# A spectral filter's weights, read four neighbours at a time

## The chip, the cores and the metric

The kernel runs on one core of a Trainium2 chip. The metric is the time of one launch on the device, in microseconds. Each engine (TensorE for matmuls, VectorE, ScalarE, GpSimd, SyncE for the DMA queue) works through its own list of instructions in order and waits on semaphores for the others. The kernel before takes 224.96 us (median of 3 runs, 224.48 to 225.21).

## The reference

One input `x` of 2048 rows by 640 columns (bfloat16) goes two ways after a layer norm, and the result is the sum of both and `x`:

```python
x = A_x
xn = layernorm(x)
X = rfft2(xn) * (w_r + 1j * w_i)          # 2048 x 321 complex filter weights
A = irfft2(X)
B = ((xn @ w_gate) * (xn @ w_up)) @ w_down   # 640 -> 1536 -> 640
out = x + A + B
```

The filter weights `w_r` and `w_i` lie in memory in the natural order of the 321 frequencies of a row.

## The kernel before, in words

The Fourier transforms are matmuls with tables of cosines and sines. The rows are split as 32 x 64 and the columns as 10 x 64, and the factor 5 of the columns is done in a few additions on VectorE. The work is cut into named tasks, and a planner written in the kernel (`_Sched.plan`) lays them out from their dependencies, priorities and estimated durations: it chooses the order on every engine, for some copies the engine too, and the PSUM banks. The estimates are those in the `task` calls; the instructions themselves are made by the functions named `em_...`. The eight PSUM banks are given out singly or in pairs; a task that reads a bank last gives it back.

The stages, roughly in this order: layer norm and transposes (T0); S, R: row additions and the first matmuls; then 16 steps t = 0 to 15, each over a group of 128 row frequencies, of which the change touches nearly all parts; then I, V: the way back, 16 groups; last the down projection (ACC, line 1141), to which the inverse transform (IV, line 1149) is added in PSUM, the sum with `x` (FIN, line 1156), and the stores. The gate and up projections (GU, line 923, ten matmuls each), their copies out of PSUM (eG) and products (H, line 938, on VectorE) have lower priority on TensorE and fill its gaps up to the end of the 16 steps and some way behind them.

One step t:

- `ld_w`: four DMAs on SyncE's queue bring 128 rows of `w_r` and of `w_i` into one of four slots.
- D (line 964, TensorE): five matmuls into a pair of PSUM banks. Column frequencies are computed as four groups k of 64, each with its real and imaginary part c, and a last group of 65 that stands for the multiples of five.
- eD (line 704, the helper that copies; ScalarE for nearly all t): PSUM to a bfloat16 row of 2 x 321, in the order c, k, m.
- C (lines 985 to 988, TensorE): four matmuls of 321 columns, along the rows.
- WM (VectorE): each of the two parts of C times `w_r` and `w_i`. Four multiplies of 256 elements (line 1000) and one of 260 (line 1003). Within a group k the 64 frequencies m come in two halves h. Frequency (k, m) of the first half is element 10 m + k + 1 of a weight row, and of the second half element 10 m + 9 - k; so neighbours along m lie ten weights apart.
- CB (lines 1018 to 1022, VectorE): sum and difference of the products to the complex result, written as bfloat16. NG (lines 1028 to 1030, ScalarE): its negated or swapped copy, so that `v_y` holds, for each k, the blocks -im, re' and im of 64 side by side.
- IA (lines 1041 and 1042, TensorE): for each of five k two matmuls, whose stationary operand is 128 neighbouring columns of `v_y`. eIA (line 704) copies the result to `v_z2w`.

The products `v_p` and `v_y` have two slots each, the rows of eD three. So C of step t waits for CB of step t-2, and IA waits for NG of its step.

In the tables below, line 704 is the line of the copy helper for ScalarE and 705 the one for VectorE; they hold the copies of all stages. Line 698 is the helper that issues DMAs.

Of the kernel before, what the change touches and what calls it, by code (L numbers as in the profile page):

```python
# [495 lines left out]
_ACTF = mybir.ActivationFunctionType  # L496
_OP = AluOpType
# [47 lines left out]
def _build(nc, A_x, A_w_r, A_w_i, B_w_gate, B_w_up, B_w_down, out, opts=None):  # L545
# [3 lines left out]
    with es:  # L549
# [64 lines left out]
        ps = es.enter_context(nc.psum_tensor("ps", [128, 8, 512], _F32))  # L614
# [14 lines left out]
        v_w = V("W").rearrange("p (r w l) -> p r w l", r=_NW, w=2)  # L629
# [5 lines left out]
        v_ti = V("TI").rearrange("p (t c n) -> p t c n", t=16, c=2)  # L635
# [14 lines left out]
        v_p = V("P").bitcast(_F32).rearrange("p (r w c l) -> p r w c l", r=2, w=2, c=2)  # L650
# [51 lines left out]
        def copy_on(c, dst, src):  # L702
            if c.e is nc.scalar:
                return c.e.activation(dst, src, _ACTF.Copy)  # L704
            return c.e.tensor_copy(dst, src)
# [241 lines left out]
        for t in range(16):  # L947
            pq = 10.0 + 0.05 * t
            ar = t % 3
            r2 = t % 2  # L950
            wr = t % _NW
            for w_ in range(2):
                for h in range(2):
                    k2 = int(_rows(t, 0, h, 0))
                    dma("ld_w%d_%d_%d" % (t, w_, h), v_w[64 * h:64 * h + 64, wr, w_, 0:321], wvs[w_][:, k2, :],
                        64 * 642, [(b_w, ("r", 4 * wr + 2 * w_ + h, 4 * wr + 2 * w_ + h + 1))], prio=9.5 + 0.05 * t,
                        semkey=("w", wr), after=[wpad])

            def em_d(c, t=t):
                bk = bank_of(c.t)  # L960
                ins = None
                for k in range(5):
                    n = 128 if k < 4 else 130
                    ins = c.e.matmul(psflat[:, bk * 512 + k * 128: bk * 512 + k * 128 + n], v_uq[:, k, t, :],
                                     v_fd[:, k * 128: k * 128 + n], start=True, stop=True)
                return ins
            td = T("D_%d" % t, "pe", 5 * _d_mm(128), em_d, reads=[(b_u, None), (b_fd, None)],
                   prio=pq, bank="pair", cls="a")

            def em_ed(c, td=td, ar=ar):  # L970
                bk = bank_of(td)
                src = psflat[:, bk * 512: bk * 512 + 642]
                dst = v_a[:, ar, :].rearrange("p (c n) -> p c n", c=2)
                copy_on(c, dst[:, :, 0:256].rearrange("p c (k m) -> p k c m", k=4),
                        src[:, 0:512].rearrange("p (k c m) -> p k c m", k=4, c=2))
                return copy_on(c, dst[:, :, 256:321], src[:, 512:642].rearrange("p (c m) -> p c m", c=2))
            ed = T("eD_%d" % t, ("act", "dve"), {"dve": _d_dve_psum(512) + _d_dve_psum(130), "act": _d_act(512) + _d_act(130)}, em_ed,
                   writes=[(b_a, ("r", ar, ar + 1))], prio=pq - 0.001, frees=td)
            hold(td, ed)

            def em_c(c, t=t, ar=ar):
                bk = bank_of(c.t)
                a_r = v_a[:, ar, 0:_LP]
                a_i = v_a[:, ar, 324:324 + _LP]
                c.e.matmul(ps[:, bk, 0:_LP], v_tf[:, t, 0, :], a_r, start=True, stop=False)
                c.e.matmul(ps[:, bk + 1, 0:_LP], v_tf[:, t, 0, :], a_i, start=True, stop=False)
                c.e.matmul(ps[:, bk, 0:_LP], v_tf[:, t, 1, :], a_i, start=False, stop=True)
                return c.e.matmul(ps[:, bk + 1, 0:_LP], v_tf[:, t, 2, :], a_r, start=False, stop=True)
            tc = T("C_%d" % t, "pe", 4 * _d_mm(_LP), em_c, reads=[(b_a, ("r", ar, ar + 1)), (b_tf, ("t", t, t + 1))],
                   prio=pq, bank="pair", cls="a")  # L990

            def em_wm(c, tc=tc, r2=r2, wr=wr):
                bk = bank_of(tc)
                ins = None
                for h in range(2):
                    xh = ps[:, bk:bk + 2, 0:256].rearrange("p c (k h m) -> p h c k m", k=4, h=2)[:, h]
                    wv = v_w[:, wr, :, 0:320].rearrange("p w (m k) -> p w k m", k=10)
                    wv = wv[:, :, 1:5, :] if h == 0 else wv[:, :, 9:5:-1, :]
                    for w in range(2):
                        c.e.tensor_tensor(  # L1000
                            v_p[:, r2, w, :, 0:256].rearrange("p c (k h m) -> p h c k m", k=4, h=2)[:, h], xh,
                            wv[:, w].unsqueeze(1).to_broadcast([128, 2, 4, 32]), _OP.mult)
                ins = c.e.tensor_tensor(  # L1003
                    v_p[:, r2, :, :, 256:321], ps[:, bk:bk + 2, 256:321].unsqueeze(1).to_broadcast([128, 2, 2, 65]),
                    v_w[:, wr, :, 0:321:5].unsqueeze(2).to_broadcast([128, 2, 2, 65]), _OP.mult)
                return ins
            wm = T("WM_%d" % t, "dve", 4 * _d_dve_psum(256) + _d_dve_psum(260), em_wm,
                   reads=[(b_w, ("r", 4 * wr, 4 * wr + 4)), (b_wp, None)],
                   writes=[(b_p, ("r", r2, r2 + 1))], prio=pq - 0.001, frees=tc)
            hold(tc, wm)  # L1010

            def em_cb(c, r2=r2):
                p00, p01, p10, p11 = (v_p[:, r2, 0, 0], v_p[:, r2, 0, 1], v_p[:, r2, 1, 0], v_p[:, r2, 1, 1])

                def k4(v):
                    return v[:, 0:256].rearrange("p (k m) -> p k m", k=4)
                ym = v_y[:, r2, 0:768].rearrange("p (k s m) -> p k s m", k=4, s=3)
                c.e.tensor_tensor(ym[:, :, 2, :], k4(p01), k4(p10), _OP.add)  # L1018
                c.e.scalar_tensor_tensor(v_y[:, r2, 896:961], p01[:, 256:321], -1.0, p10[:, 256:321], _OP.mult,
                                         _OP.subtract)  # L1020
                c.e.tensor_tensor(v_y[:, r2, 768:833], p00[:, 256:321], p11[:, 256:321], _OP.subtract)
                return c.e.tensor_tensor(ym[:, :, 1, :], k4(p00), k4(p11), _OP.subtract)  # L1022
            T("CB_%d" % t, "dve", 2 * _d_dve(256) + 2 * _d_dve(65), em_cb,
              reads=[(b_p, ("r", r2, r2 + 1))], writes=[(b_y, ("r", 2 * r2, 2 * r2 + 1))], prio=pq - 0.001)

            def em_ng(c, r2=r2):
                ym = v_y[:, r2, 0:768].rearrange("p (k s m) -> p k s m", k=4, s=3)
                c.e.activation(ym[:, :, 0, :], ym[:, :, 2, :], _ACTF.Copy, scale=-1.0)  # L1028
                c.e.activation(v_y[:, r2, 833:896], v_y[:, r2, 897:960], _ACTF.Copy, scale=-1.0)
                return c.e.activation(v_y[:, r2, 961:1024], v_y[:, r2, 769:832], _ACTF.Copy)  # L1030
            T("NG_%d" % t, "act", _d_act(256) + 2 * _d_act(63), em_ng,
              reads=[(b_y, ("r", 2 * r2, 2 * r2 + 1))], writes=[(b_y, ("r", 2 * r2 + 1, 2 * r2 + 2))],
              prio=pq - 0.001)

            def em_ia(c, t=t, r2=r2):
                bk = bank_of(c.t)
                ins = None
                for k in range(5):
                    o1, o2 = (192 * k + 64, 192 * k) if k < 4 else (768, 896)
                    dst = psflat[:, bk * 512 + k * 128: bk * 512 + (k + 1) * 128]  # L1040
                    c.e.matmul(dst, v_y[:, r2, o1:o1 + 128], v_ti[:, t, 0, :], start=True, stop=False)  # L1041
                    ins = c.e.matmul(dst, v_y[:, r2, o2:o2 + 128], v_ti[:, t, 1, :], start=False, stop=True)  # L1042
                return ins
            ia = T("IA_%d" % t, "pe", 10 * _d_mm(128), em_ia, reads=[(b_y, ("r", 2 * r2, 2 * r2 + 2)), (b_ti, None)],
                   prio=pq, bank="pair", cls="a")

            def em_eia(c, ia=ia, t=t):
                bk = bank_of(ia)
                src = psflat[:, bk * 512: bk * 512 + 640].rearrange("p (k a m) -> p k a m", k=5, a=16)
                return copy_on(c, v_z2w[:, :, :, t, :], src)  # L1050
            eia = T("eIA_%d" % t, ("act", "dve"), {"dve": _d_dve_psum(640), "act": _d_act(640)}, em_eia,
                    writes=[(b_z2, ("t", t, t + 1))], prio=pq - 0.001, frees=ia)
            hold(ia, eia)
# [3 lines left out]
        for a in range(16):  # L1057
            pa = 19.0 + 0.05 * a
            pc = 41.0 + 0.05 * a
            r2 = a % 2  # L1060
# [185 lines left out]
```

## Time and profile before

| what | value |
|---|---|
| median of the runs | 224.96 us |
| the profiled execution's own time | 224.85 us |
| its span | 222.7 us |
| TensorE busy with matmuls | 210.5 us, 95% |
| VectorE busy | 197.7 us, 89% |
| ScalarE busy | 129.4 us, 58% |
| filter multiply, line 1000 | 64 x 613 ns, 35.0 us, from 89 to 147 us |
| granted TensorE clock | 1.0 throughout |

A span runs from the first to the last instruction; the profiled execution's own time is 2.15 us longer. The profile gives for each group of instructions its line, engine, operation, output and input, their shape and count, then busy time and mean duration, then the idle time in front of it and what ended that. In a list in order of time a row is start, duration, engine, line, operation and count, with the idle time ahead of it in brackets. A row of a stretch of time gives the stretch, its length, the busy time and count of the engines, the granted clock, the DMA share and the GB/s.

### The profile page before, as it was taken

The numbers are of one execution on the slowest core, as the hardware profiler recorded it, in microseconds if no ns is written. First come the engines' busy times: TensorE is split into PE (matmuls) and PEld (weight loads), VectorE is DVE, ScalarE is ACT, GpSimd is POOL, SyncE is SP. The second block draws the span as 40 slices with busy tenths as digits, with TensorE's granted clock in tenths as the row PEclk, the third lists the DMA queues.
The fourth block names the chain that finished last, engine by engine and source line by source line (L and its number), as shares of the span: only waits on it lengthen the run. The fifth ranks groups of instructions, "written<-read, shape, count | busy, mean of one in ns | idle before, by whom it ended". The sixth has DMA issues, their size and how long they took to land.

```text
span 222.7 us, 5325 instructions
## 1 busy us (share of the span) xinstructions
PE 210.5 (95%) x2116; PEld 173.0 (78%) x2116; DVE 197.7 (89%) x535; ACT 129.4 (58%) x292; POOL 0.2 (0%) x4
## 2 busy tenths in 40 slices
PE   8999999999999999889898989989999999999995
PEld 8989899988789988667676767779876767777773
DVE  3699999999999992999999999976999999999631
ACT  2575999999998658668677876587522012200000
POOL 0000000000000000000000000000000000000000
PEclk9999999999999999999999999999999999999999
DMA  7999990000000000012121211008622223332311
GB/s 196 306 345 393 405 204 9 0 3 0 1 3 0 3 0 3 21 40 53 39 49 44 52 41 30 3 0 258 215 60 61 74 72 93 92 99 78 116 46 44
DMA packets 22184, 19.78 MB, mean 89 GB/s; under 512 B 2192, under 2 KB 21264, under 8 KB 21904
## 3 DMA queue, kind: packets, MB, share of 16 engines
q1 hardware_dynamic: 20048, 18.37, 27.6%
q10 hardware_dynamic: 2112, 1.08, 1.9%
q8 instruction: 16, 0.26, 0.5%
q14 instruction: 8, 0.07, 0.1%
HBM read 16.82 MB, written 2.62 MB: 87 GB/s over the span
## 4 chain that ended last, share of the span: by engine, by line
PE 50%; DVE 42%; DMA 2%; ACT 2%; issue 1%; SPq 0%; DVEq 0%
PE ps L923 24%; PE ps L1141 20%; DVE arena L1000 14%; DVE arena L938 3%; DVE arena L1018 3%; DVE arena L1003 2%; DMA arena<-in_A_x_dram 2%; DVE arena L1022 2%; PE ps L1068 2%; ACT arena L704 2%; PE ps L1149 2%; PE ps L813 1%; PE ps L884 1%; DVE arena L798 1%; DVE arena L837 1%
## 5 line engine op out<-in xcount | busy, mean ns | idle before, releaser
L704 ACT ACTIVATE arena<-ps 128x512 bf16<-128x512 f32 (+5 forms) x200 | 106.6, 582 | 48.7 <-PE ps L1068 26.1
L923 PE MATMUL ps<-arena 128*128 128x256 bf16 (+1 forms) x1080 | 113.6, 261 | 3.3 <-DVE arena L1003 2.7
L923 PEld LDWEIGHTS ps<-arena 128*128 128x128 bf16 x1080 | 93.3, 98 | 14.7 <-DVE arena L1003 3.7
L1141 PE MATMUL ps<-arena 128*128 128x320 bf16 x384 | 56.7, 299 | 0.0
L1141 PEld LDWEIGHTS ps<-arena 128*128 128x128 bf16 x384 | 37.3, 98 | 14.2
L1000 DVE TENSOR_TENSOR arena<-ps,arena 128x256 f32<-128x256 f32 x64 | 35.0, 613 | 0.0
L938 DVE TENSOR_TENSOR arena<-arena 128x512 bf16<-128x512 bf16 (+1 forms) x54 | 20.9, 389 | 7.3 <-ACT arena L704 7.2
L1156 DVE TENSOR_TENSOR arena<-ps,arena 128x320 bf16<-128x320 f32 x32 | 15.5, 486 | 8.1 <-PE ps L1149 8.1
L1041 PE MATMUL ps<-arena 128*128 128x128 bf16 x80 | 10.7, 219 | 2.7 <-DVE arena L1003 1.9
L1041 PEld LDWEIGHTS ps<-arena 128*128 128x128 bf16 x80 | 7.6, 97 | 5.9 <-ACT arena L704 3.1
L1028 ACT ACTIVATE arena<-arena 128x256 bf16<-128x256 bf16 x16 | 6.6, 416 | 9.4 <-DVE arena L1022 9.4
L1042 PE MATMUL ps<-arena 128*128 128x128 bf16 x80 | 10.6, 219 | 0.0
L1149 PE MATMUL ps<-arena 128*128 128x320 bf16 x32 | 9.6, 299 | 0.0
L837 DVE TENSOR_TENSOR arena<-arena 128x384 f32<-128x384 bf16 x16 | 8.9, 554 | 0.0
L1042 PEld LDWEIGHTS ps<-arena 128*128 128x128 bf16 x80 | 7.8, 98 | 0.0
L764 DVE BATCH_NORM_STATS2 arena<-arena 128x6 f32<-128x320 bf16 x8 | 3.9, 490 | 3.8 <-DMA arena<-in_A_x_dram 3.6
L1003 DVE TENSOR_TENSOR arena<-ps,arena 128x260 f32<-128x260 f32 x16 | 7.1, 441 | 0.0
L1018 DVE TENSOR_TENSOR arena<-arena 128x256 bf16<-128x256 f32 x16 | 6.8, 425 | 0.2
L813 PE MATMUL ps<-arena 128*128 128x128 bf16 x80 | 6.3, 219 | 0.6 <-ACT arena L704 0.4
L757 ACT ACTIVATE arena<-arena 128x640 bf16<-128x640 bf16 x8 | 6.8, 846 | 0.0
L1022 DVE TENSOR_TENSOR arena<-arena 128x256 bf16<-128x256 f32 x16 | 6.8, 422 | 0.0
L838 DVE TENSOR_TENSOR arena<-arena 128x256 f32<-128x256 bf16 x16 | 6.7, 421 | 0.0
(71 smaller groups left out, 224.6 us busy)
## 6 DMA issues: line engine op xcount, KB each, us to landing
arena<-in_A_x_dram SPq DMA_DIRECT2D x20, 160.0 KB, 2.9
out_dram<-arena SPq DMA_DIRECT2D x32, 80.0 KB, 1.6
arena<-in_B_w_down_dram SPq DMA_DIRECT2D x1, 1920.0 KB, 9.0
arena<-c_tf SPq DMA_DIRECT2D x4, 384.0 KB, 11.6
arena<-in_A_w_r_dram SPq DMA_DIRECT2D x32, 40.1 KB, 2.3
arena<-in_A_w_i_dram SPq DMA_DIRECT2D x32, 40.1 KB, 2.3
arena<-in_B_w_gate_dram SPq DMA_DIRECT2D x4, 320.0 KB, 7.8
arena<-in_A_x_dram SPq DMA_DIRECT2D x1, 1280.0 KB, 12.1
```

The lines of the kernel that those rows point to most:

```text
L704: return c.e.activation(dst, src, _ACTF.Copy)
L923: ins = c.e.matmul(ps[:, bk, w * n:(w + 1) * n], v_gw[:, w, j, ft, :], v_xt[:, j, rows], start=(j == 0), stop=(j == 4))
L938: return c.e.tensor_tensor(v_ht[:, ft0:ft0 + 2, rows], v_gbf[:, rr, :, 0:n], v_gbf[:, rr, :, n:2 * n], _OP.mult)
L1000: c.e.tensor_tensor(v_p[:, r2, w, :, 0:256].rearrange("p c (k h m) -> p h c k m", k=4, h=2)[:, h], xh, wv[:, w].unsqueeze(1).to_broadcast( ...
L1003: ins = c.e.tensor_tensor(v_p[:, r2, :, :, 256:321], ps[:, bk:bk + 2, 256:321].unsqueeze(1).to_broadcast([128, 2, 2, 65]), v_w[:, wr, :, 0 ...
L1018: c.e.tensor_tensor(ym[:, :, 2, :], k4(p01), k4(p10), _OP.add)
L1022: return c.e.tensor_tensor(ym[:, :, 1, :], k4(p00), k4(p11), _OP.subtract)
L1041: c.e.matmul(dst, v_y[:, r2, o1:o1 + 128], v_ti[:, t, 0, :], start=True, stop=False)
L1042: ins = c.e.matmul(dst, v_y[:, r2, o2:o2 + 128], v_ti[:, t, 1, :], start=False, stop=True)
L1141: ins = c.e.matmul(ps[:, bk, 0:320], v_ht[:, ft, a * 128:(a + 1) * 128], v_wd[:, ft, sl3], start=(ft == 0), stop=False)
L1149: return c.e.matmul(ps[:, bank_of(ag2), 0:320], v_sm[:, 2, :], v_v[:, a, sl3], start=False, stop=True)
L1156: return c.e.tensor_tensor(v_out[:, a % 2, sl3], ps[:, bk, 0:320], v_xr[:, xs, sl3], _OP.add)
```

## The change

The 256 frequencies of the four groups are kept in the order m, k instead of k, m: the four k of one m are neighbours. In that order the weights of one m are four neighbours (elements 10 m + 1 to 10 m + 4, or, for the second half, 10 m + 9 down to 10 m + 6).

- eD makes the order: it writes each part's 256 elements contiguously and reads PSUM with a step of 128 elements (512 bytes) between neighbours.
- C runs as before on the reordered columns.
- WM reads PSUM and writes the products in runs of 128, and the weights in runs of four.
- CB and NG work on unbroken runs of 256; `v_y` holds -im, re' and im as three blocks of 256.
- IA picks group k out of them with a step of four elements (8 bytes) in its stationary operand, for k = 0 to 3; the last group is contiguous as before.

No estimated duration, priority or dependency of a task is edited.

```diff
-                copy_on(c, dst[:, :, 0:256].rearrange("p c (k m) -> p k c m", k=4),
-                        src[:, 0:512].rearrange("p (k c m) -> p k c m", k=4, c=2))
+                copy_on(c, dst[:, :, 0:256].rearrange("p c (m k) -> p c m k", k=4),
+                        src[:, 0:512].rearrange("p (k c m) -> p c m k", k=4, c=2))
...
-                    xh = ps[:, bk:bk + 2, 0:256].rearrange("p c (k h m) -> p h c k m", k=4, h=2)[:, h]
-                    wv = v_w[:, wr, :, 0:320].rearrange("p w (m k) -> p w k m", k=10)
-                    wv = wv[:, :, 1:5, :] if h == 0 else wv[:, :, 9:5:-1, :]
+                    xh = ps[:, bk:bk + 2, 128 * h:128 * h + 128]
+                    wv = v_w[:, wr, :, 0:320].rearrange("p w (m k) -> p w m k", k=10)
+                    wv = wv[:, :, :, 1:5] if h == 0 else wv[:, :, :, 9:5:-1]
                     for w in range(2):
                         c.e.tensor_tensor(
-                            v_p[:, r2, w, :, 0:256].rearrange("p c (k h m) -> p h c k m", k=4, h=2)[:, h], xh,
-                            wv[:, w].unsqueeze(1).to_broadcast([128, 2, 4, 32]), _OP.mult)
+                            v_p[:, r2, w, :, 128 * h:128 * h + 128].rearrange("p c (m k) -> p c m k", k=4),
+                            xh.rearrange("p c (m k) -> p c m k", k=4), wv[:, w].unsqueeze(1).to_broadcast([128, 2, 32, 4]), _OP.mult)
...
-                c.e.tensor_tensor(ym[:, :, 2, :], k4(p01), k4(p10), _OP.add)
+                c.e.tensor_tensor(v_y[:, r2, 512:768], p01[:, 0:256], p10[:, 0:256], _OP.add)
...
-                return c.e.tensor_tensor(ym[:, :, 1, :], k4(p00), k4(p11), _OP.subtract)
+                return c.e.tensor_tensor(v_y[:, r2, 256:512], p00[:, 0:256], p11[:, 0:256], _OP.subtract)
...
-                c.e.activation(ym[:, :, 0, :], ym[:, :, 2, :], _ACTF.Copy, scale=-1.0)
+                c.e.activation(v_y[:, r2, 0:256], v_y[:, r2, 512:768], _ACTF.Copy, scale=-1.0)
...
-                    o1, o2 = (192 * k + 64, 192 * k) if k < 4 else (768, 896)
+                    if k < 4:
+                        l1, l2 = v_y[:, r2, 256 + k:768:4], v_y[:, r2, k:512:4]
+                    else:
+                        l1, l2 = v_y[:, r2, 768:896], v_y[:, r2, 896:1024]
                     dst = psflat[:, bk * 512 + k * 128: bk * 512 + (k + 1) * 128]
-                    c.e.matmul(dst, v_y[:, r2, o1:o1 + 128], v_ti[:, t, 0, :], start=True, stop=False)
-                    ins = c.e.matmul(dst, v_y[:, r2, o2:o2 + 128], v_ti[:, t, 1, :], start=False, stop=True)
+                    c.e.matmul(dst, l1, v_ti[:, t, 0, :], start=True, stop=False)
+                    ins = c.e.matmul(dst, l2, v_ti[:, t, 1, :], start=False, stop=True)
```

More of the change, by code (lines that the diff above doesn't have):

```diff
@@ L1013, in em_cb @@
                 p00, p01, p10, p11 = (v_p[:, r2, 0, 0], v_p[:, r2, 0, 1], v_p[:, r2, 1, 0], v_p[:, r2, 1, 1])
[L1015 to L1018, printed above, removed]
+                c.e.tensor_tensor(v_y[:, r2, 512:768], p01[:, 0:256], p10[:, 0:256], _OP.add)
                 c.e.scalar_tensor_tensor(v_y[:, r2, 896:961], p01[:, 256:321], -1.0, p10[:, 256:321], _OP.mult,
@@ L1026, in em_ng @@
             def em_ng(c, r2=r2):
-                ym = v_y[:, r2, 0:768].rearrange("p (k s m) -> p k s m", k=4, s=3)
-                c.e.activation(ym[:, :, 0, :], ym[:, :, 2, :], _ACTF.Copy, scale=-1.0)
+                c.e.activation(v_y[:, r2, 0:256], v_y[:, r2, 512:768], _ACTF.Copy, scale=-1.0)
                 c.e.activation(v_y[:, r2, 833:896], v_y[:, r2, 897:960], _ACTF.Copy, scale=-1.0)
```

## The prediction

> **What bounds the kernel now.** I read the page's engine totals and its chain first, then the chain in order of time, then the stretch where the chain leaves TensorE.
>
> ```profile
> PE 210.5 (95%) x2116; PEld 173.0 (78%) x2116; DVE 197.7 (89%) x535; ACT 129.4 (58%) x292; POOL 0.2 (0%) x4
> ...
> PE 50%; DVE 42%; DMA 2%; ACT 2%; issue 1%; SPq 0%; DVEq 0%
> PE ps L923 24%; PE ps L1141 20%; DVE arena L1000 14%; DVE arena L938 3%; DVE arena L1018 3%; DVE arena L1003 2%; DMA arena<-in_A_x_dram 2%; DVE arena L1022 2%; PE ps L1068 2%; ACT arena L704 2%; PE ps L1149 2%; PE ps L813 1%; PE ps L884 1%; DVE arena L798 1%; DVE arena L837 1%
> ```
>
> The averages look like TensorE's kernel. But L1000, the filter multiply in the 16 steps t, alone holds 14% of the chain, about 31 us. The first and the last four of its 64 instructions bound the stage:
>
> ```profile
> 89.27 2.18 DVE L1000 TENSOR_TENSOR arena<-ps,arena 128x256 f32<-128x256 f32 x4
> ...
> 144.79 2.19 DVE L1000 TENSOR_TENSOR arena<-ps,arena 128x256 f32<-128x256 f32 x4
> ```
>
> Between them the chain goes from one group of L1000 to the next; outside, it is mostly matmuls (L923, L1141). So this stage is bound by VectorE, and TensorE idles in it. Two steps of it on TensorE:
>
> ```profile
> 106.57 0.22 PE L1041 MATMUL ps<-arena 128*128 128x128 bf16 x1 [0.38 <-DVE arena L1003]
> ...
> 107.13 1.25 PE L923 MATMUL ps<-arena 128*128 128x256 bf16 x10
> 108.22 0.30 PE L985 MATMUL ps<-arena 128*128 128x321 bf16 x1
> ...
> 108.77 0.22 PE L1041 MATMUL ps<-arena 128*128 128x128 bf16 x1
> ...
> 109.33 0.44 PE L964 MATMUL ps<-arena 128*128 128x128 bf16 x5
> 110.23 1.26 PE L923 MATMUL ps<-arena 128*128 128x256 bf16 x10 [0.46 <-DVE arena L1003]
> 111.60 0.30 PE L985 MATMUL ps<-arena 128*128 128x321 bf16 x1
> ...
> 112.14 0.44 PE L964 MATMUL ps<-arena 128*128 128x128 bf16 x5
> 112.42 1.25 PE L923 MATMUL ps<-arena 128*128 128x256 bf16 x10
> 114.04 0.22 PE L1041 MATMUL ps<-arena 128*128 128x128 bf16 x1 [0.36 <-DVE arena L1003]
> ```
>
> Where nothing waits, starts follow each other by the true cost: a GU (ten matmuls, L923) 1.09 us (107.13 to 108.22), a C 0.55, an IA 0.56 (106.57 to 107.13), a D 0.28 (112.14 to 112.42). The waits name L1003, the last multiply of WM: its end gives back the PSUM pair that the next IA or GU needs. A bracket shows less than is lost, because the busy time counts each last matmul's drain. So I count work. From C of t=2 (93.02) to IA of t=15 (149.51), TensorE in the first four rows (L923, L1041, L985, L964 in this order) and all engines in the last:
>
> ```profile
> 93.02:149.51 56.49, 30.61 (x250) 23.39 (x250) 1.00 0.17 37
> 93.02:149.51 56.49, 10.03 (x75) 7.20 (x76) 1.00 0.17 37
> 93.02:149.51 56.49, 4.16 (x14) 1.31 (x14) 1.00 0.17 37
> 93.02:149.51 56.49, 4.86 (x55) 3.85 (x55) 1.00 0.17 37
> 93.02:149.51 56.49, 50.32 (x511) 39.94 (x512) 55.38 (x147) 41.28 (x110) 0.00 (x0) 1.00 0.17 37
> ```
>
> 25 GU x 1.09 + 15 IA x 0.56 + 14 C x 0.55 + 11 D x 0.28 = 27.3 + 8.4 + 7.7 + 3.1 = 46.5 us of work in 56.5: TensorE could give back 10.0 us here, and no more. VectorE is busy 55.4 of the 56.5, at a granted clock of 1.00 for TensorE.
>
> **WM, the multiply (L1000): removed cost.** The same shape of work with and without the large step between weights:
>
> ```profile
> L1000 DVE TENSOR_TENSOR arena<-ps,arena 128x256 f32<-128x256 f32 x64 | 35.0, 613 | 0.0
> L1003 DVE TENSOR_TENSOR arena<-ps,arena 128x260 f32<-128x260 f32 x16 | 7.1, 441 | 0.0
> L1018 DVE TENSOR_TENSOR arena<-arena 128x256 bf16<-128x256 f32 x16 | 6.8, 425 | 0.2
> L1113 DVE TENSOR_TENSOR arena<-arena 128x512 f32<-128x512 f32 x8 | 5.5, 683 | 0.0
> ```
>
> ```profile
> 111.35 2.20 DVE L1000 TENSOR_TENSOR arena<-ps,arena 128x256 f32<-128x256 f32 x4
> 113.46 0.44 DVE L1003 TENSOR_TENSOR arena<-ps,arena 128x260 f32<-128x260 f32 x1
> 113.93 0.42 DVE L1018 TENSOR_TENSOR arena<-arena 128x256 bf16<-128x256 f32 x1
> ...
> 114.54 0.42 DVE L1022 TENSOR_TENSOR arena<-arena 128x256 bf16<-128x256 f32 x1
> 114.88 0.42 DVE L938 TENSOR_TENSOR arena<-arena 128x512 bf16<-128x512 bf16 x1
> 115.21 2.18 DVE L1000 TENSOR_TENSOR arena<-ps,arena 128x256 f32<-128x256 f32 x4
> ```
>
> Records overlap, so spacing counts. Four L1000 take 2.11 us (111.35 to 113.46), 0.528 each; a 256-element operation with nothing scattered takes 0.34 (L1022, 114.54 to 114.88). L1000 steps its bf16 weights by ten elements, 20 bytes. L1003 also reads PSUM and steps its weights, by five (10 bytes), and is not slow: 441 ns for 260 elements beside 425 for 256. So the step of 20 bytes is what costs, (0.528 - 0.34)/256 = 0.73 ns an element, and neither PSUM nor stepping as such. After the change four weights lie together (8 bytes) in each 20: fewer jumps per element than L1003 makes. The bounds are 0.34 (all gone) and 0.528 (nothing gained); I take 0.34, since L1003 is the nearest row. Saved: 4 x 0.188 = 0.75 us a step, 15 times in the stretch, 11.3 us of VectorE.
>
> **CB and NG** keep their sizes; 64-element runs become 256-element ones. L1018 at 425 ns is already what it costs without gaps (by L1003's 441 for four elements more); bounds -0.01 to 0, taken as 0. The planner's durations are not edited, so every engine's order, every wait and all DMAs stay; only steps inside operands change.
>
> **eD on ScalarE, now reading PSUM 512 bytes apart per element.**
>
> ```profile
> L704 ACT ACTIVATE arena<-ps 128x512 bf16<-128x512 f32 x99 | 58.8, 600 | 15.6 <-PE ps L923 14.2 <-PE ps L964 0.8
> L704 ACT ACTIVATE arena<-ps 128x640 bf16<-128x640 f32 x32 | 21.7, 702 | 3.0 <-PE ps L1042 2.9
> L704 ACT ACTIVATE arena<-ps 128x640 f32<-128x640 f32 x15 | 9.8, 702 | 26.1 <-PE ps L1068 26.1
> ```
>
> No row shows a stepped PSUM read. The lower bound is 0 (a gain is excluded, reads and writes had 64-element runs already); the upper is L1000's price, 512 x 0.73 = 0.37 us an eD. On this engine, runs of eight (the bf16 x32 row, eR and eIA) cost the same 702 ns as unbroken ones (f32 x15), so I take 0. What hides it: D comes over 2 us before its C (D 109.33, next C 111.60), and ScalarE is free 56.5 - 41.3 = 15.2 us of the stretch. Tightened to 46.5 it has 5.2 left; 15 x 0.37 = 5.6 would eat that, so without cover it would bind (a rival below). One eD runs on VectorE ahead of the first WM (L705), where the gap behind it covers either price:
>
> ```profile
> 87.20 0.89 DVE L705 CAST arena<-ps 128x512 bf16<-128x512 f32 x2 [0.85 <-PE ps L964]
> 88.92 0.43 DVE L938 TENSOR_TENSOR arena<-arena 128x512 bf16<-128x512 bf16 x1 [0.83 <-ACT arena L704]
> ```
>
> [...]
>
> **IA, weights loaded 8 bytes apart.** Eight of the ten loads of an IA (k=0 to 3) become stepped; all stationary operands before are unbroken.
>
> ```profile
> L1041 PEld LDWEIGHTS ps<-arena 128*128 128x128 bf16 x80 | 7.6, 97 | 5.9 <-ACT arena L704 3.1 <-ACT arena L1030 2.2 <-issue 0.3
> ```
>
> An IA's ten pairs take 0.56 us, 56 ns a pair, so a load hides under the matmul before it only as long as it comes every 56 ns. Nothing covers a longer one: eight in a row. Lower bound: 56, no cost (the matmul sets it). Upper: L1000's stepped rate, 0.528 us for 256, of which about 0.08 is fixed (683 ns for 512 elements in L1113 against 425 for 256 give 1.01 ns an element, and 0.34 - 0.26 = 0.08), so 1.75 ns an element, 224 ns a load. I take no cost: the step is 8 bytes, and the nearest row (10 bytes, L1003) pays nothing. But that row passes one element in about 1.01 ns and a load 128 in 56, so this is my weakest step.
>
> [...]
>
> **The sum.** VectorE would need 56.5 - 11.3 = 45.2 us, TensorE 46.5: TensorE becomes the bound by a little. I walked one cycle of four steps (99.19 to 114.04, 14.85 us) by these spacings: between two WM ends TensorE has 3.0 us of work, VectorE 2.8 without an H (L938) and 3.0 to 3.1 with one; every C is done about 1 us before its WM. I end at about 12.3 against 12.06 of TensorE work, so some 0.25 a cycle stays, 0.9 over 3.8 cycles, and I leave 0.3 for waits on NG. Gain 10.0 - 1.2 = 8.8. Behind IA of t=15 TensorE's order is the same, and the load of w_down (issued at 150.27, after the last IA) moves with it:
>
> ```profile
> 150.27 0.39 SPq L698 DMA_DIRECT2D arena<-in_B_w_down_dram  x1
> 121.29 1.10 SPq L698 DMA_DIRECT2D arena<-in_A_w_r_dram  x2
> 122.44 1.24 SPq L698 DMA_DIRECT2D arena<-in_A_w_i_dram  x2
> ```
>
> The filter loads take SP 2.34 us a step, inside the new 3.0. The profiled execution took 224.85 us for a span of 222.7; 222.7 - 8.8 + 2.15 = 216.05, and the median of the runs lies 0.11 above it: **216.2 us**, own range 214.8 to 217.5.
>
> **Rivals.**
> *ScalarE pays for the stepped read* (0.37 an eD). For: every element jumps. Against: the engine shows no such cost for short runs. ScalarE then needs 41.3 + 5.6 = 46.9 with waits in strict order, about 2 us more lost: 218.2.
> *Stepped loads lose their cover in part.* L1003 passes 10 bytes in 1.01 ns, 9.9 bytes per ns, without loss; a load now spans 1024 bytes, 103 ns at that rate. 8 x 47 = 0.38 an IA, 6.0 in all. Of the 10.0 us of idle time 4.0 stay, less some 0.3 of waits: 221.3. Against: the port need not be like VectorE's.
> *Stepped loads cost what L1000's weights do* (the slower one). 224 ns: 8 x 0.168 x 16 = 21.5 us, against 10.0 of idle time: 236.5. It decides from the point where 128 loads eat those 10.0 us: 78 ns more each, 134 ns a load. Against: 8 bytes is below L1003's 10.
> *The multiply hardly gains*, because runs of four still jump: at half the price saved VectorE needs 50.9, gain 5: 220; with nothing saved, 225.
>
> **How the numbers follow.** Forecast 0.43, ScalarE 0.20, loads in part 0.16, loads slower than before 0.13, multiply 0.08. The likeliest is 216.2. The range 214.5 to 224 leaves out the slower loads, the end of the last case and a little below: about 2 in 10. A change of 0.3%, 0.7 us, is what a measurement here can tell: faster 0.81, the same 0.06 (tails of the loads in part and of the multiply), slower 0.13.
>
> **What would show it.** L1000 near 430 ns a record; eD's row (128x512 from L704) at 600, or near 970 by its rival; IA pairs at 56 ns and their load row at 97, or more by the other rivals; TensorE's waits on L1003 gone and the stretch near 48 us. If L1000 falls while IA grows beyond 1.2 us, the forecast is wrong on the loads; if L1000 stays above 520, on the step.

## The result and the profile after

The changed kernel takes 214.33 us (median of 4 runs, 214.27 to 215.15), the kernel before beside it 225.09 us. The ratio is 0.9535, with a 95% interval of 0.9505 to 0.9564. The forecast was 216.2 us; the median lies 0.17 us below the low end of the range, 214.5, and 0.5 below the forecast's own range of 214.8 to 217.5.

The page of the changed kernel, engine totals and chain. CB, NG, IA and all that follows have moved up by one to four lines; IA is now lines 1040 and 1041, NG begins at 1024, ACC is 1140.

```profile
PE 207.1 (97%) x2116; PEld 174.9 (82%) x2116; DVE 185.8 (87%) x535; ACT 128.5 (60%) x292; POOL 0.2 (0%) x4
...
PE 79%; DVE 17%; ACT 1%; issue 1%; DVEq 0%
PE ps L923 38%; PE ps L1140 21%; PE ps L731 3%; PE ps L1041 2%; PE ps L1040 2%; PE ps L1067 2%; PE ps L964 2%; DVE arena L938 2%; PE ps L1148 2%; PE ps L884 1%; DVE arena L837 1%; PE ps L813 1%; DVE arena L798 1%; PE ps L985 1%; PE ps L988 1%; PE ps L987 1%
```

L1000, 14% of the chain before, is nowhere in it now. VectorE's share fell from 42% to 17%, TensorE's rose from 50% to 79%. The groups that the change touches, one shape each (line, engine, operation, count, then busy time and mean ns of one, then idle time ahead):

```profile
L1000 DVE TENSOR_TENSOR arena<-ps,arena 128x256 f32<-128x256 f32 x64 | 22.6, 418 | 0.0
L1003 DVE TENSOR_TENSOR arena<-ps,arena 128x260 f32<-128x260 f32 x16 | 7.1, 444 | 0.0
L1015 DVE TENSOR_TENSOR arena<-arena 128x256 bf16<-128x256 f32 x16 | 6.8, 423 | 0.2
L704 ACT ACTIVATE arena<-ps 128x512 bf16<-128x512 f32 x99 | 59.0, 602 | 16.0 <-PE ps L923 14.3 <-PE ps L964 0.8
L1040 PEld LDWEIGHTS ps<-arena 128*128 128x128 bf16 x80 | 8.8, 112 | 0.4
```

The multiply fell from 613 to 418 ns. ScalarE's copies of this size, of which 15 are eD, stayed (602 beside 600). The row of IA's loads shows 112 ns instead of 97; it is a mean of 64 stepped loads and the 16 unbroken ones of the last group, so a stepped load takes about 116 (an estimate: (80 x 112 - 16 x 97) / 64). The stretch from C of t=2 to IA of t=15, whose 56.49 us held 46.5 us of TensorE work, with the same columns as in the prediction:

```profile
92.83:139.36 46.53, 46.53 (x514) 41.18 (x512) 44.22 (x147) 40.42 (x110) 0.00 (x0) 1.00 0.21 44
```

It takes 46.53 us now, and TensorE is busy all the time. That saves 9.96 of the 10.1 us by which the span fell (222.7 to 212.6). Part of TensorE's order in it, GU, C, D, GU, IA, GU, the tasks that the prediction showed with waits between them:

```profile
106.39 1.26 PE L923 MATMUL ps<-arena 128*128 128x256 bf16 x10
107.48 0.30 PE L985 MATMUL ps<-arena 128*128 128x321 bf16 x1
...
108.03 0.44 PE L964 MATMUL ps<-arena 128*128 128x128 bf16 x5
108.30 1.25 PE L923 MATMUL ps<-arena 128*128 128x256 bf16 x10
109.40 0.22 PE L1040 MATMUL ps<-arena 128*128 128x128 bf16 x1
...
109.95 1.26 PE L923 MATMUL ps<-arena 128*128 128x256 bf16 x10
```

No bracket is left: every task starts where the one before ends its issue (GU 1.09, IA 109.40 to 109.95, 0.55). The waits for L1003 are gone from TensorE's list of waits, which has 2.5 us in all, none of them in this stretch:

```profile
PE ps L731 <- DVE arena L738: 1.0, 1, 1.0
PE ps L923 <- ACT arena L704: 0.8, 2, 0.6
PE ps L1067 <- DVE arena L1099: 0.5, 1, 0.5
PE ps L884 <- DVE arena L871: 0.2, 1, 0.2
```

### The profile page after: what moved, and what is told of

Same layout as the page of the kernel before. It is cut to its first block, busy times and chain, and to the rows that moved or that the text cites. A ratio compares the mean times of both kernels' runs of the same rounds, so it can differ in the third digit from the quotient of the medians.

```text
span 212.6 us, 5325 instructions
## 1 busy us (share of the span) xinstructions
PE 207.1 (97%) x2116; PEld 174.9 (82%) x2116; DVE 185.8 (87%) x535; ACT 128.5 (60%) x292; POOL 0.2 (0%) x4
## 4 chain that ended last, share of the span: by engine, by line
PE 79%; DVE 17%; ACT 1%; issue 1%; DVEq 0%
PE ps L923 38%; PE ps L1140 21%; PE ps L731 3%; PE ps L1041 2%; PE ps L1040 2%; PE ps L1067 2%; PE ps L964 2%; DVE arena L938 2%; PE ps L1148 2%; PE ps L884 1%; DVE arena L837 1%; PE ps L813 1%; DVE arena L798 1%; PE ps L985 1%; PE ps L988 1%; PE ps L987 1%
## 5 line engine op out<-in xcount | busy, mean ns | idle before, releaser
L923 PEld LDWEIGHTS ps<-arena 128*128 128x128 bf16 x1080 | 93.6, 98 | 11.3 <-ACT arena L704 1.9
L1140 PEld LDWEIGHTS ps<-arena 128*128 128x128 bf16 x384 | 37.3, 98 | 14.2
L1000 DVE TENSOR_TENSOR arena<-ps,arena 128x256 f32<-128x256 f32 x64 | 22.6, 418 | 0.0
L1040 PEld LDWEIGHTS ps<-arena 128*128 128x128 bf16 x80 | 8.8, 112 | 0.4
L1041 PEld LDWEIGHTS ps<-arena 128*128 128x128 bf16 x80 | 8.7, 113 | 0.1
L1003 DVE TENSOR_TENSOR arena<-ps,arena 128x260 f32<-128x260 f32 x16 | 7.1, 444 | 0.0
L731 PEld LDWEIGHTS ps<-arena 128*128 128x128 bf16 x56 | 5.9, 150 | 1.0 <-DVE arena L738 1.0
```

Source lines behind the costliest of these rows:

```text
L731: ins = c.e.matmul(ps[:, bk + (i % 2), (i % 4) * 128:(i % 4 + 1) * 128], v_dum[:, 0:128], v_dum[:, 128:256], start=True, stop=True)
L923: ins = c.e.matmul(ps[:, bk, w * n:(w + 1) * n], v_gw[:, w, j, ft, :], v_xt[:, j, rows], start=(j == 0), stop=(j == 4))
L1000: c.e.tensor_tensor(v_p[:, r2, w, :, 128 * h:128 * h + 128].rearrange("p c (m k) -> p c m k", k=4), xh.rearrange("p c (m k) -> p c m k", k ...
L1003: ins = c.e.tensor_tensor(v_p[:, r2, :, :, 256:321], ps[:, bk:bk + 2, 256:321].unsqueeze(1).to_broadcast([128, 2, 2, 65]), v_w[:, wr, :, 0 ...
L1040: c.e.matmul(dst, l1, v_ti[:, t, 0, :], start=True, stop=False)
L1041: ins = c.e.matmul(dst, l2, v_ti[:, t, 1, :], start=False, stop=True)
```

## The experiments

The theory: the step of 20 bytes between weights is the whole cost of the slow multiply; VectorE gets quicker by 0.75 us a step, until TensorE's own work binds. Rivals: the longer runs in PSUM, CB and NG bring a part; VectorE still binds; the steps that the change adds elsewhere (PSUM reads, weight loads) cost something that the gain covers up.

**One cause alone: weights without a step.** The kernel before, with unbroken weights in the multiply:

```diff
                     wv = v_w[:, wr, :, 0:320].rearrange("p w (m k) -> p w k m", k=10)
-                    wv = wv[:, :, 1:5, :] if h == 0 else wv[:, :, 9:5:-1, :]
+                    wv = v_w[:, wr, :, 128 * h:128 * h + 128].rearrange("p w (k m) -> p w k m", k=4)
```

> The kernel before, only that the multiply reads 128 neighbouring weights per half instead of weights ten apart (so it uses the weights of other frequencies; all else, also the order in PSUM, CB, NG and IA, is as before). Theory (the 20-byte step between weights is the whole cost, and TensorE's work is the limit behind it): L1000 falls from 613 to about 418 ns and the time to about that of the changed kernel, 214.3 us, within 0.5. Rival (unbroken runs in PSUM, CB and NG bring part of the gain): L1000 stays above 450 ns or the time above 215.5.

Measured: 214.26 us, ratio to the kernel before 0.9542 (0.9527 to 0.9557), with L1000 at

```profile
L1000 DVE TENSOR_TENSOR arena<-ps,arena 128x256 f32<-128x256 f32 x64 | 22.6, 415 | 0.0
```

The weights' step explains the whole gain: eD, CB, NG and IA are those of the kernel before here, and the stretch from C of t=2 to IA of t=15 takes 46.50 us. Runs of four are also as good as unbroken weights (418 beside 415 ns).

**Half of the saving.** The kernel before, with unbroken weights for the second half alone:

```diff
-                    wv = wv[:, :, 1:5, :] if h == 0 else wv[:, :, 9:5:-1, :]
+                    wv = wv[:, :, 1:5, :]
+                    if h == 1:
+                        wv = v_w[:, wr, :, 128:256].rearrange("p w (k m) -> p w k m", k=4)
```

> The kernel before, with 128 neighbouring weights for the second half of the frequencies only (wrong weights there); the first half keeps the step of ten. Half of VectorE's saving, 16 x 0.375 = 6.0 us. Theory (VectorE binds until it falls under TensorE's 46.5 us of the stretch): VectorE needs 56.5 - 5.6 = 50.9 and still binds, so all of the half saving arrives: 224.96 - 6 = 219 us, 218.5 to 220, and the second half brings less, 4 to 5. Rival (gain in proportion to the saving, nothing caps it): both halves bring the same. Rival (TensorE's order already fits from a small saving on): under 217.

Measured: 219.3 us, ratio 0.9769 (0.9747 to 0.9791), 5.4 us less than the 224.67 of the kernel before beside it. The second half brings 219.3 - 214.26 = 5.0 us. In the times the gap between the halves (5.4 and 5.0) is within what these runs can tell. The stretch from C of t=2 to IA of t=15 tells them apart better:

```profile
92.99:144.03 51.04, 49.93 (x514) 40.00 (x513) 49.58 (x148) 41.54 (x110) 0.00 (x0) 1.00 0.20 40
```

It goes from 56.49 over 51.04 to 46.50 us, so the halves bring 5.45 and 4.54 of the 5.6 that each saves on VectorE. The first arrives nearly whole, and TensorE's 46.5 us of work cut off about one from the second. These are single profiles; the next run shows the cap itself.

**Less work for VectorE on top.** From t=2 on, the changed kernel without the multiply of 260 and without the two 65-element operations of CB:

```diff
+                if t >= 2:
+                    return ins
                 ins = c.e.tensor_tensor(
                     v_p[:, r2, :, :, 256:321], ps[:, bk:bk + 2, 256:321].unsqueeze(1).to_broadcast([128, 2, 2, 65]),
...
+                if t < 2:
+                    c.e.scalar_tensor_tensor(v_y[:, r2, 896:961], p01[:, 256:321], -1.0, p10[:, 256:321], _OP.mult,
+                                             _OP.subtract)
+                    c.e.tensor_tensor(v_y[:, r2, 768:833], p00[:, 256:321], p11[:, 256:321], _OP.subtract)
```

> The changed kernel with less work for VectorE: from t=2 on, the multiply of 260 (L1003) and the two 65-element operations of CB are left out (the last group of frequencies is then not filtered), about 0.35 + 0.27 = 0.62 us a step, 8.7 us in 14 steps. Theory (TensorE's work binds the 16 steps now): no gain beyond 0.5 us, 213.8 to 214.4. Rival (VectorE still binds, both were cut together): up to 8 us less, at least under 212.

Measured: 214.52 us, ratio 0.9548 (0.9524 to 0.9572): nothing gained, and 0.1 us above the times expected. The stage as one row, with VectorE third:

```profile
93.00:139.00 46.00, 46.00 (x509) 41.04 (x507) 35.81 (x104) 39.98 (x110) 0.00 (x0) 1.00 0.22 44
```

VectorE is busy 35.8 of 46 us instead of 44.2 of 46.5, and TensorE all 46. After the change TensorE's work is the limit in this stage, and a further microsecond saved on VectorE is worth nothing.

**VectorE makes the order.** The changed kernel with eD as before and the step in the multiply's read of PSUM:

```diff
...
-                    xh = ps[:, bk:bk + 2, 128 * h:128 * h + 128]
+                    xh = ps[:, bk:bk + 2, 0:256].rearrange("p c (k h m) -> p h c m k", k=4, h=2)[:, h]
...
```

> The changed kernel, only that ScalarE copies D in the order it had before and VectorE's multiply makes the new order by reading PSUM with a step of 64 elements (256 bytes) per element; the weights are read four at a time, and the result is the same. Theory (a step in PSUM costs nothing on ScalarE, 602 ns against 600, and a step in SBUF of over 16 bytes costs VectorE 0.73 ns an element): if PSUM is as free for VectorE, L1000 stays at 418 ns and the time at 214.3. Rival (for VectorE a jump per element costs the same in PSUM as in SBUF): L1000 near 613 ns and the time near 225.

Measured: 214.47 us, ratio 0.9554 (0.9533 to 0.9575), and

```profile
L1000 DVE TENSOR_TENSOR arena<-ps,arena 128x256 f32<-128x256 f32 x64 | 22.6, 416 | 0.0
```

A step of 256 bytes from one element to the next costs VectorE nothing when it reads PSUM (416 ns beside 418), while 20 bytes in SBUF cost it 195 ns (613 beside 418). Which engine makes the order on its PSUM side makes no difference here (214.47 us beside 214.33).

**ScalarE writes with the step.** The changed kernel with eD's step on the other side:

```diff
-                copy_on(c, dst[:, :, 0:256].rearrange("p c (m k) -> p c m k", k=4),
-                        src[:, 0:512].rearrange("p (k c m) -> p c m k", k=4, c=2))
+                copy_on(c, dst[:, :, 0:256].rearrange("p c (m k) -> p k c m", k=4),
+                        src[:, 0:512].rearrange("p (k c m) -> p k c m", k=4, c=2))
```

> The changed kernel, only that ScalarE makes the order on the other side: it reads PSUM contiguously and writes every fourth bfloat16 element (8 bytes apart); the result is the same. Theory (a step under about 10 bytes in SBUF is free, as it was for the multiply's 260-element neighbour): eD's 512-element record stays near 600 ns, and even 0.37 us more would hide under ScalarE's slack: 214.3, within 0.6. Rival (writes of single 2-byte elements cost ScalarE an extra cycle each): record near 1000 ns and the time 215 to 218.

Measured: 220.18 us, ratio 0.9799 (0.9767 to 0.9832). The theory's number was wrong, and the rival's record and time were too low. An eD in order of time, the stretch from C of t=2 to IA of t=15 with ScalarE fourth, the engines of the chain, and who makes TensorE wait:

```profile
103.79 1.34 ACT L704 ACTIVATE arena<-ps 128x512 bf16<-128x512 f32 x1
```

```profile
95.20:145.79 50.59, 48.51 (x513) 40.48 (x511) 43.96 (x145) 46.49 (x110) 0.00 (x0) 1.00 0.20 39
```

```profile
PE 60%; DVE 18%; ACT 15%; DMA 4%; SPq 1%; issue 1%; DVEq 0%
```

```profile
PE ps L1040 <- ACT arena L1026: 1.5, 5, 0.3
```

An eD takes 1.34 us instead of 0.60. In the stretch ScalarE is busy for 46.5 us instead of 40.4, as long as TensorE's 46.5 us of work; IA waits for NG (L1026), which stands behind the copies in ScalarE's order. ScalarE's share of the chain grows from 1% to 15%, most of it between 91 and 129 us, where the chain runs through its copies and NG. So ScalarE sets the pace for most of the steps. From the first D to IA of t=15 they take 58.9 us instead of 53.1, as much more as the whole kernel; the side on which the order is made decides over half of the gain: 214.3 against 220.2. The one eD that VectorE makes pays too, 1321 ns where the same row of the changed kernel has 691:

```profile
L705 DVE CAST arena<-ps 128x512 bf16<-128x512 f32 x1 | 1.3, 1321 | 0.8 <-PE ps L964 0.8
```

**How long a run ScalarE must write.** eD's 512 elements as two copies of 256, with another order for each third of the steps:

```diff
+                elif t % 3 == 0:
+                    for cc in range(2):
+                        c.e.activation(dst[:, cc, 0:256].rearrange("p (m k q) -> p k m q", k=4, q=2),
+                                       src[:, 0:512].rearrange("p (k c m q) -> p c k m q", k=4, c=2, q=2)[:, cc], _ACTF.Copy)
...
+                else:
+                    for cc in range(2):
+                        c.e.activation(dst[:, cc, 0:256].rearrange("p (m k) -> p k m", k=4),
+                                       src[:, 0:512].rearrange("p (k c m) -> p c k m", k=4, c=2)[:, cc], _ACTF.Copy)
```

> The run in which ScalarE wrote every fourth element took 1.34 to 1.37 us for 512 elements instead of 0.60. Here eD's 512 elements are split into two copies of 256 that write, by step t, runs of two neighbours 16 bytes apart (line 980), runs of four 32 bytes apart (line 984) and single elements 8 bytes apart (line 988, the order of the changed kernel; in the other two the frequencies come in another order, so they are filtered with other weights). An unbroken copy of 256 takes 384 ns. Theory (ScalarE pays about 1.5 ns for each write that doesn't continue the last one): singles about 765 ns, pairs about 575, fours about 480. Rival (only writes of less than 4 bytes are slow): singles about 765, pairs and fours near 384. Rival (a price per new piece of 16 bytes, as VectorE's reads): pairs at least as slow as singles.

Measured in one profile (a call is listed by its first line, so 979, 983 and 987; the first row is an unbroken copy of the same size):

```profile
L704 ACT ACTIVATE arena<-ps 128x256 bf16<-128x256 f32 x24 | 9.0, 383 | 2.1 <-PE ps L923 1.6
L979 ACT ACTIVATE arena<-ps 128x256 bf16<-128x256 f32 x12 | 4.1, 405 | 0.8 <-PE ps L964 0.8
L983 ACT ACTIVATE arena<-ps 128x256 bf16<-128x256 f32 x10 | 3.4, 403 | 0.1
L987 ACT ACTIVATE arena<-ps 128x256 bf16<-128x256 f32 x8 | 5.4, 818 | 0.1
```

Single 2-byte elements cost 818 ns, pairs 405, fours 403, unbroken 383. The theory (a price per jump) and the rival by 16-byte pieces both fall; the rival by which only writes of less than 4 bytes are slow fits: lone 2-byte writes cost 1.7 ns more an element, pairs and fours some 20 ns a record.

**Longer steps in the weight loads.** IA's stepped operand from another buffer, with 16 and with 64 bytes between elements (below the first; the second has 4096 and 32):

```diff
-                        l1, l2 = v_y[:, r2, 256 + k:768:4], v_y[:, r2, k:512:4]
+                        xl = v_xt[:, 0:1, :].rearrange("p j s -> p (j s)")
+                        l1, l2 = xl[:, k:1024:8], xl[:, k + 4:1024:8]
```

> The changed kernel, only that the eight stepped loads of an IA take every eighth element (16 bytes apart) of another buffer that nothing writes in this stage (so the last transform gets other data). TensorE binds the stage, so each ns that 128 loads are longer than their cover shows in the time. Theory (the load takes columns at its own rate whatever the step): load record 112 ns as with 8 bytes, pairs every 56 ns, 214.3 us. Rival (the loads' port pays by the distance it passes, 10 bytes per ns): 2048 bytes, 205 ns, 19 us more, 233. Between them: the record grows above 112 and the pairs to 60 to 110 ns.

> As the run with 16 bytes, with every 32nd element (64 bytes apart). Theory (own rate whatever the step): 112 ns and 214.3 us. Rival (by distance): 8192 bytes, over 800 ns a load, more than 300 us in all. Rival (one price for every load whose elements lie in different 16-byte pieces): the same as with 16 bytes.

Measured: 215.04 us (ratio 0.9574, 0.9537 to 0.961) and 215.18 us (0.9569, 0.9541 to 0.9597). Load rows, first with 16, then with 64 bytes:

```profile
L1041 PEld LDWEIGHTS ps<-arena 128*128 128x128 bf16 x80 | 10.0, 139 | 0.4
```

```profile
L1041 PEld LDWEIGHTS ps<-arena 128*128 128x128 bf16 x80 | 10.1, 140 | 0.4
```

By the starts in order of time, the ten pairs of an IA span 0.50 to 0.51 us from first to last with 4-element steps, as before the change, 0.54 to 0.56 with 16 bytes and 0.55 to 0.58 with 64. So 8-byte steps lengthen the record (97 to 112 ns in the row) and hide wholly; 16 bytes add about 5 ns a pair; beyond that the distance hardly matters. The rival by distance falls by far, and so does the theory that the step is without any effect; the middle case, one price from 16 bytes on, fits. The stretch from C of t=2 to IA of t=15 grows from 46.53 to 47.12 and 47.24 us, 0.04 to 0.05 an IA; the medians, 0.7 and 0.85 us over the changed kernel's, agree, though they are hardly outside what these runs can tell. In both runs the buffer changed with the step, so a share of the buffer in the 5 ns is not excluded.

**Which step costs the multiply.** The kernel before with four steps, one for each multiply, on lines 1001 (12 bytes), 1003 (16), 1005 (18) and 1008 (pairs every 20):

```diff
+                def wstep(w, s):
+                    return v_w[:, wr, w, 0:32 * s].rearrange("p (m k) -> p k m", k=s)[:, 0:4, :]
...
+                c.e.tensor_tensor(part(v_p[:, r2, 0, :, 0:256], 0), x0,
+                                  wstep(0, 6).unsqueeze(1).to_broadcast([128, 2, 4, 32]), _OP.mult)
...
+                wp = v_w[:, wr].rearrange("p w l -> p (w l)")[:, 0:640].rearrange("p (n k) -> p n k", k=10)[:, :, 1:3]
```

> The kernel before with four different steps in the four multiplies of 256, each on its own line (other weights, so other results): 12 bytes, 16 bytes, 18 bytes, and pairs of neighbours every 20 bytes. The 10-byte step was free (441 ns for 260), the 20-byte step cost 613. Theory (VectorE pays about 1.75 ns for each new piece of 16 bytes, or 1.01 ns an element if that is more): 12 bytes 256 x 0.75 x 1.75 = 0.336 us against 0.26, so about 495 ns; 16 and 18 bytes about 613; pairs at 20 bytes about 420 to 430. Rival (the price rises in proportion to the distance): 16 bytes about 535 and 18 bytes about 575. Rival (a price per jump over 10 bytes): 12 bytes at 613 already, pairs about 515.

Measured in one profile:

```profile
L1005 DVE TENSOR_TENSOR arena<-ps,arena 128x256 f32<-128x256 f32 x16 | 9.9, 618 | 0.0
L1003 DVE TENSOR_TENSOR arena<-ps,arena 128x256 f32<-128x256 f32 x16 | 9.7, 608 | 0.0
L1001 DVE TENSOR_TENSOR arena<-ps,arena 128x256 f32<-128x256 f32 x16 | 7.9, 495 | 0.0
L1008 DVE TENSOR_TENSOR arena<-ps,arena 128x256 f32<-128x256 f32 x16 | 7.0, 437 | 0.0
```

12 bytes 495 ns, 16 bytes 608, 18 bytes 618, pairs 437: the theory had 495, 613, 613 and 420 to 430. Proportion to distance and a price per jump both fall. The rows fit a price of about 1.75 ns for each new piece of 16 bytes (an estimate from the 20-byte step: 528 ns a multiply by spacing, less 80 fixed, for 256 elements), or about 1 ns an element (683 ns for 512 against 425 for 256) if that is more. That is a fit to these rows; what in the hardware lies behind it was not shown. By that price the 10-byte step is not quite free: it makes five new pieces for eight elements, 1.09 ns an element, some 20 ns more for 260 elements than unbroken ones (an estimate). That fits L1003's 441 ns beside the 415 of 256 unbroken ones, and pairs every 20 bytes, with as many pieces, at 437.

## Why the prediction was right, point by point

The mechanism, the step of 20 bytes and the new bound, was right. The time came out just under the range because one term of the sum, the waits that stay, was too large, and because the time outside the span happened to be shorter.

- **The bound.** Right, and shown: cutting VectorE's multiply alone moves the time (214.26 with unit weights), and cutting VectorE further does not (214.52).
- **The multiply, 0.528 to 0.34 us by spacing.** Right: 613 to 418 ns a record, a fall of 195 where 188 was taken. The choice of L1003 as the nearest row is borne out by the run with four steps: by its fit, steps of five elements, 10 bytes, make five new 16-byte pieces for eight elements, four neighbours in 20 bytes fewer still. By the fit L1003 was itself some 20 ns short of free, which the comparison with L1018 (425 ns, with other operands) did not show.
- **CB and NG at no gain.** Right: the first operation of CB takes 423 ns where it took 425.
- **eD at no cost.** Right (602 ns; the run with unit weights, whose eD is that of the kernel before, has 602 too), but partly by luck: the row with runs of eight said nothing of stepped reads, and when ScalarE makes the same order by its writes it costs 0.74 us an eD. "ScalarE pays for the stepped read" is refuted. Reads of PSUM 512 bytes apart on ScalarE (602 ns beside 600) and 256 apart on VectorE (416 beside the changed kernel's 418) are both free here.
- **IA's loads at no cost.** Right in the time: pairs every 56 ns, although the mean record grew by 15 ns. "Loads in part" and "loads slower" are refuted by this pace: a stepped load's record, about 116 ns, is longer than the 103 of the first rival and still costs nothing. So the length of the record did not decide. Even 64 bytes apart add only some 5 ns a pair, so the rate that "loads in part" took from VectorE, 9.9 bytes per ns, does not hold for these loads: at that rate the 8192 bytes that such a load passes would take over 800 ns.
- **TensorE's work, 46.5 us.** Right to 0.1: 46.53.
- **The sum, 8.8 us of gain.** Too small; the span fell by 10.1. The step that failed is the 1.2 us taken off for waits that stay (0.9 for four-step cycles of 12.3, 0.3 for NG). The walked cycle, from an IA to the IA four steps on, runs in the changed kernel from 97.28 to 109.40 and takes 12.12 us, 0.06 over the 12.06 of work:

```profile
97.28 0.22 PE L1040 MATMUL ps<-arena 128*128 128x128 bf16 x1
...
109.40 0.22 PE L1040 MATMUL ps<-arena 128*128 128x128 bf16 x1
```

  TensorE waits for neither VectorE nor NG anywhere in the stretch, so both parts of the 1.2 us should have been nothing. Why the walk went wrong is argued, not shown: it began from a state in which TensorE waits for VectorE, counted 0.25 us of waiting in one cycle, and multiplied that by 3.8 cycles, though a TensorE that has once fallen behind finds its inputs ready. The span accounts for 1.3 of the 1.9 us between forecast and median. The rest is in the time outside the span, taken as 2.15 from the one profiled execution plus 0.11, while the four runs of the changed kernel show 1.8 to 2.6; that part is chance.
- **Behind the stage.** Right: the load of w_down is issued 10.2 us earlier than at 150.27, as the last IA moved, and nothing behind was lost.

```profile
140.11 0.39 SPq L698 DMA_DIRECT2D arena<-in_B_w_down_dram  x1
```

## What to carry to other kernels

Judge an engine's share stage by stage: a kernel at 95% of one engine had 10 us to give where another engine bound it, and the starts of tasks (not the busy time) told how much to 0.1 us. Compare the rows of one operation in two layouts before blaming its size: a slow row beside a quick one of the same count names the operand to rearrange. When an order must be changed, put the step on the side where it was free here (a PSUM read, 602 ns beside 600 on ScalarE; a weight load with 8 bytes between elements, pairs every 56 ns in either case) and keep ScalarE's writes of 2-byte elements unbroken, or at least in pairs (383 and 405 ns for 256 elements, 818 for lone ones).

## What the runs showed of the hardware that was not expected

- ScalarE writes lone 2-byte elements in SBUF at less than half its rate (818 against 383 ns for 256 elements), and pairs at nearly the full one (405). VectorE's one such copy took 1321 ns instead of 691 for 512.
- VectorE's read of 2-byte weights fits one price over steps of 10 to 20 bytes, about 1.75 ns for each new piece of 16 bytes (the estimate above): 441 ns (260 elements, 10 bytes), 495 (12), 608 (16), 618 (18), 613 (20), beside 415 unbroken.
- PSUM reads by ScalarE and VectorE took no notice of steps of 512 and 256 bytes (602 and 416 ns, beside 600 and 415 without).
- A stepped weight load has a longer record (row means 97 ns unbroken; 112 at 8 bytes, 139 at 16, 140 at 64, each with 16 unbroken loads among 80), but almost none of it reaches the pace of the matmuls (pairs every 56 ns unbroken and at 8 bytes, some 5 ns more at 16 and 64). Why the record grows while the pace hardly does was not tried.
